# Attention and gated MLP on one core: a common PSUM pool, paced weight conversion, and unsplit float32 probabilities for the first 256 queries of each head in the first batch

## The chip, the cores and the metric

One core of a Trainium2 chip runs the whole program. The metric is device time in microseconds of one execution; lower is better. Engines are called PE (TensorE), DVE (VectorE), ACT (ScalarE), POOL (GpSimd) and SP (SyncE, which issues the DMAs); each works through its own list of instructions in order.

## What is computed

All inputs are float32 (the weights come as 64-bit numbers and are made float32 on the chip). Queries are averaged in pairs, so a head has 576 queries against 1152 keys of 64 elements.

```python
batch, n_heads, seq, head_dim = (4, 8, 1152, 64)
n_tokens, d_model, d_ff = (2304, 512, 1536)
q_pool = q.reshape(B, H, S // factor, factor, D).mean(axis=3)      # factor = 2
scores = scale * np.matmul(q_pool, k.transpose(0, 1, 3, 2))
scores = scores - np.max(scores, axis=-1, keepdims=True)
attn = np.exp(scores)
attn = attn / (np.sum(attn, axis=-1, keepdims=True) + 1e-09)
...                                          # x = attn @ v, heads side by side
gate = 1.0 / (1.0 + np.exp(-(x @ w_gate)))
return (gate * (x @ w_val)) @ w_out
```

## The kernel before, in words

**Precision by splitting.** A value is split into a rounded part (float32r) and the rest, and a product is made of several float32r matmuls: two for scores, two for a product with the values (the stationary operand `vt` holds the values' high and low parts side by side in 128 columns), three for the gated MLP. Splitting costs an ACT (or POOL) copy for the high part and a DVE or POOL subtraction for the low one.

**Steps of the attention.** Two heads are a pair (`p`, 16 pairs in 4 batches) and make nine steps (`STEPS`, L157), each a tile of 128 queries: four of the first head, one with 64 queries of each, four of the second. `PB` = 36 steps are a batch. A step (`scores`, L303) is: three cuts of the scores on PE (L326), the row maximum on DVE (L333), the exponential on ACT (L338) into `P`; then nine PE transposes in three groups (L367), each copied as its high part by ACT (L382) and subtracted for its low part by DVE (L386) into `pt`. When a head's 256 or 320 queries are there, `values` (L395) multiplies: 18 matmuls (L408); the halves in 64 partitions each are added by an ACT copy (L419) into `t` and a DVE addition (L422) into `y`. After a pair, `normalise` (L432) multiplies `y` by the inverse sums (DVE L464) and splits it into `x` (ACT L472, POOL L476). `head_operands` (L233) loads and splits q, k and v.

**PSUM.** Eight banks of 512 columns. In the first batch scores alternate between `S0` (banks 0, 1 and a quarter of 2) and `S1` (the rest of 2, bank 3, half of 4); later only `S0` is used. Transposes have the two banks `T` (6, 7), results of products have `m` (3, 4, 5), of which two are taken away (`blocked`) until the last exponential of the first batch.

**The rest.** `convert` (L483) makes float32 parts of a weight piece: a load on SP, ACT L493, DVE L497, L498, L503, ACT L507, POOL L510, a store to DRAM; 36 pieces, from the first steps on. `gated` (L527) of batch b runs beside the attention of batch b+1: 864 matmuls a batch (L541), with weights loaded back (L555, L601). The gated product of the first batch can't begin before the first batch's last `x` is there, so PE has nothing but attention until then.

**What sets the order.** Every piece is recorded as an operation with an engine, an assumed duration, a priority (about its step) and the buffers that it takes (`SLOTS` gives their number). `Plan.run` (L63) plays them against each other by the assumed durations: an engine that is free takes the operation of lowest priority number that could start. The resulting list is then written out, engine by engine; the assumed durations decide the order and nothing else.

Of the kernel before, what the change touches and what calls it, by code (L numbers as in the profile page):

```python
# [37 lines left out]
class Plan:  # L38


    LAT = {"PE": 0.22, "ACT": 0.12, "DVE": 0.12, "POOL": 0.15, "SP": 0.0}
# [21 lines left out]
    def run(self):  # L63
# [32 lines left out]
        while done < len(self.ops):  # L96
            if not times:
                left = sorted((o.key[0], o.eng) for e in ready for _, o in ready[e])
                raise RuntimeError(f"planner stuck at {t}: {left[:10]} {nxt}")
            t = heapq.heappop(times)  # L100
            while times and times[0] <= t + 1e-9:
                heapq.heappop(times)
            again = True
            while again:
                again = False
                for e in self.LAT:
                    if busy[e] > t + 1e-9:
                        continue
                    put, pick = [], None
# [39 lines left out]
def attention_glu_kernel(ctx: ExitStack, tc: tile.TileContext, qT, kT, vt_in, v, wg, wv, wo, out):  # L149
# [15 lines left out]
    }  # L165
    pl = Plan(SLOTS, ("m",))
# [5 lines left out]
    def tiles(tag, shape, dt, pool=const):  # L172
# [12 lines left out]
        "m": [bank[:, 512 * i:512 * i + 512] for i in (3, 4, 5)],  # L185
        "T": [bank[:, 512 * i:512 * i + 512] for i in (6, 7)],
# [10 lines left out]
        "g": tiles("g", [128, 2, HALF], F32R),  # L197
        "opart": tiles("opart", [128, HALF], F32),
# [6 lines left out]
    }  # L205
    w_d = {
# [11 lines left out]
    def act(n, extra=0):  # L218
        return 0.17 + 0.815e-3 * n + 0.093 * extra

    def dve(n):
        return 0.14 + 1.06e-3 * n

    def pool(n, two=True):
        return 0.2 + (2.4e-3 if two else 1.3e-3) * n

    def dma(kb):
        return 0.1 + kb / 250

    T_PE = 0.12  # L230


    def head_operands(u, need):  # L233
# [67 lines left out]
        return dict(k=kh, q=qh, v=vh, got=got, vg=vg)  # L301

    def scores(p, j, hd, st):  # L303
# [15 lines left out]
        cuts = ((0, 384), (384, 896), (896, SK)) if early and s % 2 else ((0, 512), (512, 1024), (1024, SK))  # L319
        for n, (a, b) in enumerate(cuts):  # L320

            def mm(a=a, b=b):
                t = tl(sh)
                seq = [(q, kk[w][:, a:b]) for w, q in lhs for kk in (KA, KB)]
                for n, (q, k) in enumerate(seq):
                    nc.tensor.matmul(out=t[:, a:b], lhsT=q, rhs=k, start=(n == 0), stop=(n == len(seq) - 1))  # L326

            mms.append(pl.op("PE", 2 * len(lhs) * pe(b - a), mm, s - 0.5, after=got if n == 0 else mms[-1:],
                             uses=uses + ([sh] if n else []), take=[] if n else [sh]))
# [12 lines left out]
        a = pl.op("DVE", dve(SK), rmax, s - 0.5, after=mms[-1:], uses=[sh])  # L342
# [4 lines left out]
        ex_op = pl.op("ACT", act(SK, 2), ex, s - 0.5, after=[a], uses=block + [sh] + ([] if j == 0 else [st["den"]]), take=take)  # L347
        st.setdefault("ex", []).append(ex_op)

# [7 lines left out]
        for w, g, _, _ in dst:  # L357
            if (w, g) not in st:
                st[w, g] = dict(h=pl.hold("pt"), ops=[])
                new.append(st[w, g]["h"])  # L360
        for n in range(3):
            th = pl.hold("T")
# [6 lines left out]
            a = pl.op("PE", 3 * T_PE, tr, s + 1 + 0.1 * n, after=[ex_op], uses=[ph], take=[th])  # L369
            for w, g, so, do in dst:  # L370
# [4 lines left out]
                def views(n=n, th=th, so=so, do=do, h=h, width=width):  # L375
                    src = tl(th)[:, 0:384].rearrange("p (c q) -> p c q", q=128)[:, :, so:so + width]
                    d = tl(h)[:, :, 3 * n:3 * n + 3, do:do + width]
                    return src, d[:, 0], d[:, 1]
# [9 lines left out]
                tk = [h] if h in new else []  # L388
                if tk:
                    new.remove(h)  # L390
                b = pl.op("ACT", act(3 * width), hi, s + 1 + 0.1 * n, after=[a], uses=[th] + ([] if tk else [h]), take=tk)
                b = pl.op("DVE", dve(3 * width), lo, s + 1 + 0.1 * n, after=[b], uses=[th, h])
                st[w, g]["ops"].append(b)

    def values(p, j, w, g, hd, st):  # L395
# [5 lines left out]
        m = pl.hold("m")  # L401
        last = None
        for n, (c0, c1) in enumerate(((0, 3), (3, 5), (5, 7), (7, 9))):

            def mm(c0=c0, c1=c1):
                for c in range(c0, c1):
                    for k in range(2):
                        nc.tensor.matmul(out=tl(m)[:, 0:N], lhsT=tl(hd[w]["v"])[:, c], rhs=tl(h)[:, k, c, 0:N],  # L408
                                         start=(c == 0 and k == 0), stop=(c == NC - 1 and k == 1))

            last = pl.op("PE", 2 * (c1 - c0) * pe(N), mm, s, after=st[w, g]["ops"] + [hd[w]["vg"]] + in_turn if n == 0 else [last],
                         uses=[h, hd[w]["v"]] + ([m] if n else []), take=[] if n else [m])
            if n == 0:
                in_turn[:] = [last]
        th = pl.hold("t")
        mine, other = slice(64 * w, 64 * w + 64), slice(64 - 64 * w, 128 - 64 * w)

# [5 lines left out]

        last = pl.op("ACT", act(N), cp, s, after=[last], uses=[m], take=[th])
        tk = []
        if "y" not in st:
            st["y"] = pl.hold("y")
            tk = [st["y"]]
        st.setdefault("yo", []).append(
            pl.op("DVE", dve(N), add, s, after=[last], uses=[m, th] + ([] if tk else [st["y"]]), take=tk))  # L430

    def normalise(p, st):  # L432
# [16 lines left out]
        ms = [pl.hold("m"), pl.hold("m")]  # L449
# [33 lines left out]
    def convert(kind, m, s, due):  # L483
# [11 lines left out]
        def bits():  # L495
            low, high = tl(cr)[:, :, 0], tl(cr)[:, :, 1]
            nc.vector.tensor_scalar(out=low, in0=low, scalar1=29, scalar2=None, op0=ALU.logical_shift_right)  # L497
# [18 lines left out]
        a = pl.op("SP", dma(512), load, due - 4, take=[cr], late=3.0)  # L516
        a = pl.op("ACT", act(512), scale, due, after=[a], uses=[cr])
        a = pl.op("DVE", 2 * dve(512), bits, due, after=[a], uses=[cr])
        a = pl.op("DVE", dve(512), join, due, after=[a], uses=[cr])
# [7 lines left out]
    def gated(b, xs):  # L527
        base = PB * (b + 1) + 2.5
# [3 lines left out]
        def product(at, w, parts, N, uses, after):  # L532

            m = pl.hold("m")
# [13 lines left out]
        for th in range(3):  # L548
            gs = {}
            for m_ in range(4 * th, 4 * th + 4):  # L550
# [7 lines left out]
                lw = pl.op("SP", dma(1024), load, at - 4, after=stored["wg", m_], take=[wh], late=3.0)  # L558
                for n in range(2):
                    sg, gh = pl.hold("sg"), pl.hold("g")  # L560
                    qc = slice(n * HALF, (n + 1) * HALF)
                    for s in range(2):
# [15 lines left out]
                        else:  # L578
# [13 lines left out]
                            a = pl.op("ACT", act(HALF), hi, at - 1, after=[a], uses=[sg], take=[gh])  # L592
                            a = pl.op("POOL", pool(HALF), lo, at - 1, after=[a], uses=[sg, gh])
                            gs[m_ % 4, n] = (gh, a)
            for dm in range(4):
# [8 lines left out]
                lw = pl.op("SP", dma(512), load, at - 4, after=stored["wo", m_], take=[wh], late=3.0)  # L604
                for n in range(2):
# [21 lines left out]
                    if th == 0:  # L627
                        a = pl.op("ACT", act(HALF), post, at - 1, after=[last], uses=[ms], take=[oh])
# [11 lines left out]
    in_turn = []  # L640
    acc = {}
    xs = {}
    blocked = [pl.hold("m"), pl.hold("m")]
    pl.op("SP", 0.0, lambda: None, -100, take=blocked)
    for b in range(B):
# [60 lines left out]
```

## Time and profile before

| | |
|---|---|
| runs before | 1060.4 us median of 3 (1058.04 to 1060.67) |
| profiled execution | 1058.06 us, of which the span of its instructions is 1056.2 us |
| PE busy | 981.1 us (93%), 6944 matmuls |
| DVE, ACT, POOL busy | 654.6 us (62%), 561.3 us (53%), 423.7 us (40%) |
| first row maximum, 36th row maximum, first gated matmul start at | 14.31 us, 198.46 us, 226.57 us |
| bytes moved by DMA | 166.33 MB, 157 GB/s in the mean |

Read it by stages: the shares over the span mix a stage in which PE waits with one in which it does not. A matmul's duration in the profile holds its way through the array, and matmuls overlap; what one costs in a run of them is the distance from one to the next, which the chain of waits shows as a piece's length over its count.

### The profile page before, as it was taken

The page shows a single profiled execution, that of the slowest core. Times are in us where ns is not written, and L with a number is a line of the kernel's source. Part 1 is how long each engine was busy: PE and PEld are TensorE (multiplying, and loading weights), DVE is VectorE, ACT ScalarE, POOL GpSimd, SP SyncE. Part 2 cuts the span into 40 slices and gives each one's busy share as a digit, 9 for nine tenths or more (in the row PEclk, how much of TensorE's full clock was granted, in tenths as well). Part 3 has the DMA queues.
Part 4 walks back from the last instruction along what each step waited for, and adds up shares of the span by engine and source line. Part 5 has one row for each costly group of instructions (what it writes and reads, how often), then busy time and mean ns, then how long its engine had stood idle before and what let it go on. Part 6 is the DMA issues. An engine that isn't in the chain of part 4 may idle for free.

```text
span 1056.2 us, 18322 instructions
## 1 busy us (share of the span) xinstructions
PE 981.1 (93%) x6944; PEld 931.3 (88%) x6944; DVE 654.6 (62%) x1086; ACT 561.3 (53%) x1179; POOL 423.7 (40%) x408
## 2 busy tenths in 40 slices
PE   4886777679999999999999999999999999999998
PEld 3675666569999999999999999999999999999998
DVE  4778887777778887865656665665656665530121
ACT  4657665566666656655555545545555545522211
POOL 6445544435646455624524434414524422111211
PEclk9889988999999999999999999999999999999999
DMA  6645555636777585874444352554444332255443
GB/s 164 188 145 168 146 165 149 162 129 198 224 240 229 164 238 173 266 239 136 137 125 136 116 157 103 153 154 136 137 125 137 121 108 80 87 159 168 170 175 92
DMA packets 53463, 166.33 MB, mean 157 GB/s; under 512 B 10368, under 2 KB 14464, under 8 KB 47232
## 3 DMA queue, kind: packets, MB, share of 16 engines
q1 hardware_dynamic: 53376, 165.18, 51.1%
q8 instruction: 54, 0.88, 0.4%
q14 instruction: 33, 0.27, 0.1%
HBM read 141.56 MB, written 23.59 MB: 156 GB/s over the span
## 4 chain that ended last, share of the span: by engine, by line
PE 76%; DVE 3%; ACT 1%; issue 1%; DMA 0%; ACTq 0%; DVEq 0%
PE bank L541 43%; PE bank L326 12%; PE bank L408 11%; PE bank L367 10%; PE bank L455 1%; DVE cr L503 1%; DVE cr L498 1%; DVE pt L386 1%; DVE nm L333 1%; ACT P L338 0%; ACT pt L382 0%; DVE cr L497 0%; DMA wo<-wo_d 0%; ACT cr L493 0%; DVE sg L581 0%
## 5 line engine op out<-in xcount | busy, mean ns | idle before, releaser
L541 PE MATMUL bank<-x,wg 128*128 128x288 f32 x2304 | 369.4, 303 | 0.0
L541 PEld LDWEIGHTS bank<-x,wg 128*128 128x128 f32 x2304 | 316.2, 188 | 0.1
L386 DVE TENSOR_TENSOR pt<-bank,pt 128x384 fp32r<-128x384 f32 (+1 forms) x480 | 233.1, 510 | 122.6 <-ACT pt L382 120.7
L382 ACT ACTIVATE pt<-bank 128x384 fp32r<-128x384 f32 (+1 forms) x480 | 206.9, 460 | 121.3 <-PE bank L367 115.1
L367 PE MATMUL bank<-ident,P 128*128 128x128 f32 x1296 | 214.1, 280 | 34.4 <-DVE pt L386 31.4
L333 DVE TENSOR_REDUCE nm<-bank 128x1 f32<-128x1152 f32 x144 | 195.1, 1355 | 63.4 <-PE bank L326 60.4
L367 PEld LDWEIGHTS bank<-ident,P 128*128 128x128 f32 x1296 | 161.0, 143 | 50.4 <-DVE pt L386 40.4
L326 PE MATMUL bank<-KA,Q 128*128 128x512 f32 (+3 forms) x480 | 177.5, 371 | 27.9 <-ACT P L338 12.5
L338 ACT ACTIVATE P<-bank,nm 128x1152 f32<-128x1152 f32 x144 | 175.8, 1221 | 50.5 <-DVE nm L333 43.0
L541 PE MATMUL bank<-g,wo 128*128 128x288 f32 x1152 | 183.8, 303 | 1.3 <-DMA wo<-wo_d 1.3
L588 POOL TENSOR_TENSOR g<-sg,g 128x288 fp32r<-128x288 f32 x96 | 77.5, 807 | 264.9 <-ACT g L585 259.3
L408 PE MATMUL bank<-pt,vt 128*128 128x256 f32 (+1 forms) x1152 | 168.8, 301 | 0.0
L326 PE MATMUL bank<-KB,Q 128*128 128x512 f32 (+3 forms) x480 | 165.9, 365 | 1.0 <-POOL KB L286 1.0
L541 PEld LDWEIGHTS bank<-g,wo 128*128 128x128 f32 x1152 | 158.6, 189 | 2.1 <-DVE opart L625 1.5
L408 PEld LDWEIGHTS bank<-pt,vt 128*128 128x128 f32 x1152 | 160.2, 193 | 0.1
L326 PEld LDWEIGHTS bank<-KA,Q 128*128 128x128 f32 x480 | 94.3, 196 | 47.0 <-ACT P L338 17.7
L326 PEld LDWEIGHTS bank<-KB,Q 128*128 128x128 f32 x480 | 94.8, 197 | 13.1 <-POOL KB L286 2.2
L581 DVE SCALAR_TENSOR_TENSOR sg<-sg,bank 128x288 f32<-128x288 f32 x96 | 43.3, 451 | 94.6 <-PE bank L541 93.2
L286 POOL TENSOR_TENSOR KB<-kr,KA 128x576 fp32r<-128x576 f32 x64 | 96.9, 1515 | 5.9 <-ACT KA L281 1.9
L575 ACT ACTIVATE sg<-bank 128x288 f32<-128x288 f32 x96 | 39.6, 412 | 106.8 <-PE bank L541 102.9
L510 POOL TENSOR_TENSOR cs<-cr,cs 128x512 fp32r<-128x512 f32 x36 | 50.9, 1415 | 92.3 <-ACT cs L507 88.5
L293 POOL CAST vt<-vr 128x576 fp32r<-128x576 f32 x32 | 23.1, 721 | 138.2 <-PE bank L408 138.2
(35 smaller groups left out, 613.0 us busy)
## 6 DMA issues: line engine op xcount, KB each, us to landing
wg<-wg_d SPq DMA_DIRECT2D x48, 1024.0 KB, 4.9
wo<-wo_d SPq DMA_DIRECT2D x48, 512.0 KB, 3.6
kr<-in_kT_dram SPq DMA_DIRECT2D x64, 288.0 KB, 5.1
wg_d<-cs SPq DMA_DIRECT2D x24, 512.0 KB, 6.0
qr<-in_qT_dram SPq DMA_DIRECT2D x32, 288.0 KB, 3.9
vr<-in_v_dram SPq DMA_DIRECT2D x32, 288.0 KB, 3.4
qr<-in_qT_dram SPq DMA_DIRECT2D x32, 256.0 KB, 3.6
cr<-in_wg_dram SPq DMA_DIRECT2D x12, 512.0 KB, 5.2
```

The lines of the kernel that those rows point to most:

```text
L286: nc.gpsimd.tensor_tensor(out=kb[:, s], in0=tl(kr)[:, s], in1=ka[:, s].bitcast(F32), op=ALU.subtract)
L326: nc.tensor.matmul(out=t[:, a:b], lhsT=q, rhs=k, start=(n == 0), stop=(n == len(seq) - 1))
L333: nc.vector.tensor_reduce(out=c, in_=tl(sh)[:, 0:SK], axis=AXX, op=ALU.max, negate=True)
L338: nc.scalar.activation(out=tl(ph), in_=tl(sh)[:, 0:SK], func=ACTF.Exp, bias=c, accum_out=tl(st["den"])[:, col:col + 1])
L367: nc.tensor.transpose(out=tl(th)[:, c * 128:(c + 1) * 128], in_=tl(ph)[:, k:k + 128], identity=ident)
L382: nc.scalar.activation(out=dh, in_=src, func=ACTF.Copy)
L386: nc.vector.tensor_tensor(out=dl, in0=src, in1=dh.bitcast(F32), op=ALU.subtract)
L408: nc.tensor.matmul(out=tl(m)[:, 0:N], lhsT=tl(hd[w]["v"])[:, c], rhs=tl(h)[:, k, c, 0:N], start=(c == 0 and k == 0), stop=(c == NC - 1 and ...
L510: nc.gpsimd.tensor_tensor(out=tl(cs)[:, 1], in0=tl(cr)[:, :, 0].bitcast(F32), in1=tl(cs)[:, 0].bitcast(F32), op=ALU.subtract)
L541: nc.tensor.matmul(out=ps[:, 0:N], lhsT=l, rhs=r, start=(n == 0 and j == 0), stop=(n == 3 and j == 2))
L581: nc.vector.scalar_tensor_tensor(out=tl(sg), in0=tl(sg), scalar=1.0, in1=tl(ms)[:, 0:HALF], op0=ALU.add, op1=ALU.mult)
L588: nc.gpsimd.tensor_tensor(out=tl(gh)[:, 1], in0=tl(sg), in1=tl(gh)[:, 0].bitcast(F32), op=ALU.subtract)
```

## The change

The planner's table of assumed durations is set anew, and a free engine other than PE now leaves an operation for a more urgent one that will be ready within 0.4 us (`WAIT`). PSUM: `T` and `m` become one pool `b` of banks 3 to 7 (two of them blocked in the first batch as before, so three are in use there); bank 2, which `S0` and `S1` share, is a buffer `b2` of its own, and a step on `S1` now makes its cut in bank 2 last. In the first batch the first 256 queries of each head (`g == 0`) keep their transposed probabilities unsplit in `pe` (float32): no low part is made, and the product is nine float32 matmuls with the raw values `vr` as the stationary operand (64 columns), whose result ACT copies straight into `y`. The other 320 queries, and all later batches, stay split. Weight pieces get later due steps in the first batch, and a load waits for the exponential eight steps ahead of its due step. `kr` and `vr` have two buffers; `x`, `g`, `sg` and `t` have one fewer, and `g` and `opart` take the place of `pe` after the first batch.

```diff
 class Plan:
+    WAIT = 0.4
...
+                        if t < o.at <= t + self.WAIT and can(o, o.at):
+                            soon.append(o)
                         put.append(it)
+                    if pick and e != "PE" and any(
+                        t + pick.dur > u.at + self.WAIT and u.prio < pick.prio - 0.3 for u in soon
+                    ):
+                        heapq.heappush(ready[e], it)
+                        pick = None
...
-        "S0": 1, "S1": 1, "T": 2, "m": 3, ... "P": 2, "pt": 2,
-        "vr": 1, "vt": 2, "y": 2, "t": 2, "rb": 1, "x": 7, "g": 9, ...
-        "cr": 2, "kr": 1, "cs": 1, "sg": 3, "den": 2,
+        "S0": 1, "S1": 1, "b2": 1, "b": 5, ... "P": 2, "pt": 2, "pe": 2,
+        "vr": 2, "vt": 2, "y": 2, "t": 1, "rb": 1, "x": 6, "g": 8, ...
+        "cr": 2, "kr": 2, "cs": 1, "sg": 2, "den": 2,
...
-        cuts = ((0, 384), (384, 896), (896, SK)) if early and s % 2 else ((0, 512), (512, 1024), (1024, SK))
+        cuts = ((384, 896), (896, SK), (0, 384)) if early and s % 2 else ((0, 512), (512, 1024), (1024, SK))
+        shared = [pl.hold("b2")] if early else []
...
-                st[w, g] = dict(h=pl.hold("pt"), ops=[])
+                st[w, g] = dict(h=pl.hold("pe" if s < PB and g == 0 else "pt"), ops=[])
...
+                b = pl.op("ACT", act(3 * width), hi, s + 1 + 0.1 * n, after=[a], uses=[th, h])
+                if h.tag == "pt":
+                    b = pl.op("DVE", dve(3 * width), lo, s + 1 + 0.1 * n, after=[b], uses=[th, h])
...
+        whole = h.tag == "pe"
+        vh = hd[w]["vr" if whole else "v"]
+        for n in range(NC):
+            def mm(c=n):
+                if whole:
+                    nc.tensor.matmul(out=tl(m)[0:D, 0:N], lhsT=tl(vh)[:, c], rhs=tl(h)[:, c, 0:N],
+                                     start=(c == 0), stop=(c == NC - 1))
+                else:
+                    for k in range(2):
+                        nc.tensor.matmul(out=tl(m)[:, 0:N], lhsT=tl(vh)[:, c], rhs=tl(h)[:, k, c, 0:N], ...)
...
+        def cp_whole():
+            nc.scalar.activation(out=tl(st["y"])[mine, a:b], in_=tl(m)[0:D, 0:N], func=ACTF.Copy)
...
         a = pl.op("SP", dma(512), load, due - 4, take=[cr], late=3.0)
+        gate.append((a, max(0, int(due) - AHEAD)))
...
-                    due = max(due, 6 + 2.5 * (k + 8 * th))
+                    due = max(due, 16 + 2.5 * (k + 8 * th))
...
+    for o, k in gate:
+        o.after.append(exs[k])
```

The order that comes out differs on every engine; two places follow. Names are tile and buffer number; `bank` is all of PSUM.

On PE, the first head's product of its first 256 queries. Before (`pt`, `vt`), between the scores of two steps:

```order
L326 MATMUL bank<-KB_69,Q_71 128x128
L408 MATMUL bank<-pt_76,vt_79 128x256 x18
L367 MATMUL bank<-ident,P_74 128x128 x6
L326 MATMUL bank<-KA_67,Q_71 128x384
L326 MATMUL bank<-KB_69,Q_71 128x384
L326 MATMUL bank<-KA_67,Q_71 128x512
```

With the change (`pe`, `vr`):

```order
L346 MATMUL bank<-KB_68,Q_70 128x256
L437 MATMUL bank<-pe_107,vr_79 64x256 x3
L346 MATMUL bank<-KA_66,Q_70 128x384
L346 MATMUL bank<-KB_68,Q_70 128x384
L437 MATMUL bank<-pe_107,vr_79 64x256 x6
L388 MATMUL bank<-ident,P_75 128x128 x6
```

It is nine instructions in place of 18, comes a step sooner (in the fourth step, not after the fifth), and is parted by the step's cut in bank 2 (128x384), which on this odd step now comes last.

On DVE, from the first row maximum (`nm`) on. Before:

```order
L333 TENSOR_REDUCE nm<-bank 128x1 x2
L503 SCALAR_TENSOR_TENSOR cr_114<-cr_114 128x512
L497 TENSOR_SCALAR cr_115<-cr_115 128x512
L498 SCALAR_TENSOR_TENSOR cr_115<-cr_115 128x512
L386 TENSOR_TENSOR pt_76<-bank,pt_76 128x3x128
L333 TENSOR_REDUCE nm<-bank 128x1
L270 SCALAR_TENSOR_TENSOR Q_71<-qr_73,Q_71 64x576
L386 TENSOR_TENSOR pt_76<-bank,pt_76 128x3x128 x2
```

With the change:

```order
L353 TENSOR_REDUCE nm<-bank 128x1 x2
L288 SCALAR_TENSOR_TENSOR Q_71<-qr_74,Q_71 64x576
L353 TENSOR_REDUCE nm<-bank 128x1 x2
L411 TENSOR_TENSOR pt_77<-bank,pt_77 128x3x128 x3
L353 TENSOR_REDUCE nm<-bank 128x1
L411 TENSOR_TENSOR pt_77<-bank,pt_77 128x3x128 x2
```

The low parts of the first two steps are gone, and so is the conversion of weights (`cr`), whose first piece now stands after the eleventh row maximum.

## Rows read from the trace of the kernel before

**Rows 1.** The page's busy time of each engine, with its share of the span and its number of instructions.

```profile
PE 981.1 (93%) x6944; PEld 931.3 (88%) x6944; DVE 654.6 (62%) x1086; ACT 561.3 (53%) x1179; POOL 423.7 (40%) x408
```

**Rows 2.** Windows: each stretch (us), its length, busy time of the engines in it with their instructions, PE's granted clock as a share of 2.4 GHz, busy share of the DMA engines, GB/s. The borders are the start of the first row maximum, of the 36th, and of the first gated matmul, then 262, 464 and 935 us.

```profile
0.00:14.31 14.31, 3.92 (x9) 2.59 (x10) 3.29 (x5) 4.62 (x6) 6.93 (x11) 1.00 0.88 227
14.31:198.46 184.15, 136.54 (x773) 114.87 (x773) 145.54 (x223) 112.37 (x226) 91.55 (x79) 0.89 0.53 153
198.46:226.57 28.11, 20.11 (x131) 17.42 (x131) 21.67 (x36) 17.87 (x36) 13.69 (x14) 0.98 0.63 175
226.57:262.00 35.43, 32.50 (x237) 30.98 (x237) 26.92 (x39) 21.43 (x46) 16.10 (x15) 1.00 0.56 159
262.00:464.00 202.00, 200.20 (x1464) 192.91 (x1463) 159.96 (x260) 128.52 (x266) 106.15 (x97) 1.00 0.71 223
464.00:935.00 471.00, 471.00 (x3459) 456.13 (x3458) 278.02 (x484) 252.54 (x545) 168.47 (x170) 1.00 0.42 129
935.00:1056.20 121.20, 116.85 (x881) 116.41 (x879) 19.16 (x42) 23.99 (x57) 20.80 (x25) 1.00 0.45 153
```

**Rows 3.** The timeline (start in us, length in us, engine, line, instruction): the first and the 36th row maximum on DVE, the last `y` of the first batch, the first gated matmuls.

```profile
14.31 2.64 DVE L333 TENSOR_REDUCE nm<-bank 128x1 f32<-128x1152 f32 x2 [1.40 <-PE bank L326]
198.46 1.36 DVE L333 TENSOR_REDUCE nm<-bank 128x1 f32<-128x1152 f32 x1 [0.75 <-PE bank L326]
222.98 1.11 DVE L464 TENSOR_TENSOR y<-y,bank 128x256 f32<-128x256 f32 x4
226.57 1.66 PE L541 MATMUL bank<-x,wg 128*128 128x288 f32 x11
```

**Rows 4.** Waits from 14.31 to 198.46 us: who waited for whom, us in total, times, the longest.

```profile
ACT pt L382 <- PE bank L367: 39.1, 33, 3.2
PEld bank L367 <- DVE pt L386: 29.0, 33, 4.0
PE bank L367 <- DVE pt L386: 22.1, 18, 3.8
DVE nm L333 <- PE bank L326: 16.3, 15, 2.6
DVE pt L386 <- ACT pt L382: 14.0, 14, 1.4
PE bank L326 <- ACT P L338: 10.3, 12, 2.5
```

**Rows 5.** Instructions of DVE and ACT from 14.31 to 198.46 us by line and shape: busy us, mean ns of one, then the idle time before them and what ended it.

```profile
L333 DVE TENSOR_REDUCE nm<-bank 128x1 f32<-128x1152 f32 x35 | 47.3, 1353 | 18.6 <-PE bank L326 16.3 <-ACT P L338 2.2
L386 DVE TENSOR_TENSOR pt<-bank,pt 128x384 fp32r<-128x384 f32 x85 | 44.7, 549 | 11.0 <-ACT pt L382 10.3
L503 DVE SCALAR_TENSOR_TENSOR cr<-cr 128x512 uint32<-128x512 uint32 x14 | 13.5, 962 | 0.2
L498 DVE SCALAR_TENSOR_TENSOR cr<-cr 128x512 uint32<-128x512 uint32 x13 | 12.2, 941 | 1.1
L422 DVE TENSOR_TENSOR y<-bank,t 64x256 f32<-64x256 f32 x7 | 2.9, 418 | 0.9 <-ACT t L419 0.7
L422 DVE TENSOR_TENSOR y<-bank,t 64x320 f32<-64x320 f32 x6 | 2.9, 488 | 2.2 <-ACT t L419 2.2
L382 ACT ACTIVATE pt<-bank 128x384 fp32r<-128x384 f32 x85 | 40.0, 490 | 36.8 <-PE bank L367 36.4
L419 ACT ACTIVATE t<-bank 64x256 f32<-64x256 f32 x7 | 2.7, 380 | 3.5 <-PE bank L408 3.4
```

**Rows 6.** Pieces of the chain of waits, in order of time: start, length, what. A run of matmuls of one line is one piece: 18 of 320 columns twice, 12 of the gated product, 18 of 256 columns, three transposes.

```profile
198.43 3.31 PE bank L408 x18
...
208.95 2.65 PE bank L408 x18
...
231.17 1.59 PE bank L541 x12
232.75 2.17 PE bank L408 x18
...
248.42 0.33 PE bank L367 x3
```

**Rows 7.** The products with the values over the whole span: matmuls and their weight loads (count, busy us, mean ns of one, idle before).

```profile
L408 PE MATMUL bank<-pt,vt 128*128 128x256 f32 (+1 forms) x1152 | 168.8, 301 | 0.0
L408 PEld LDWEIGHTS bank<-pt,vt 128*128 128x128 f32 x1152 | 160.2, 193 | 0.1
```

**Rows 8.** The timeline around one odd step on `S1`: the exponential of the step before, the cut in bank 2 that waits for it, the last cut, the row maximum.

```profile
40.24 1.22 ACT L338 ACTIVATE P<-bank,nm 128x1152 f32<-128x1152 f32 x1 [0.69 <-DVE nm L333]
...
41.61 0.44 PE L326 MATMUL bank<-KA,Q 128*128 128x384 f32 x1 [0.39 <-ACT P L338]
41.89 0.34 PE L326 MATMUL bank<-KB,Q 128*128 128x384 f32 x1
...
42.65 0.31 PE L326 MATMUL bank<-KB,Q 128*128 128x256 f32 x1
...
43.09 1.35 DVE L333 TENSOR_REDUCE nm<-bank 128x1 f32<-128x1152 f32 x1
```

More of the change, by code (lines that the diff above doesn't have):

```diff
@@ L108, in run @@
                         continue
-                    put, pick = [], None
+                    put, pick, soon = [], None, []
                     while ready[e]:
@@ L184, in attention_glu_kernel @@
         "S1": [bank[:, SK:2 * SK]],
-        "m": [bank[:, 512 * i:512 * i + 512] for i in (3, 4, 5)],
-        "T": [bank[:, 512 * i:512 * i + 512] for i in (6, 7)],
+        "b": [bank[:, 512 * i:512 * i + 512] for i in (3, 4, 5, 6, 7)],
         "kr": tiles("kr", [128, SK], F32),
@@ L205, in attention_glu_kernel, with change_pools @@
     }
+    late = ctx.enter_context(ExitStack())
+    early = ctx.enter_context(ExitStack())
+    TL["pe"] = tiles("pe", [128, NC, 256], F32, early.enter_context(tc.tile_pool(name="pe", bufs=1)))
+    def change_pools():
+        early.close()
+        pool = late.enter_context(tc.tile_pool(name="late", bufs=1))
+        TL["g"] = tiles("g", [128, 2, HALF], F32R, pool)
+        TL["opart"] = tiles("opart", [128, HALF], F32, pool)
     w_d = {
@@ L341, in scores @@
         block = [] if not early else [blocked[0], blocked[1]]
-        a = pl.op("DVE", dve(SK), rmax, s - 0.5, after=mms[-1:], uses=[sh])
+        a = pl.op("DVE", dve(SK), rmax, s - 0.5, after=mms[-1:], uses=[sh] + shared)
         take = [ph]
@@ L346, in scores @@
             take.append(st["den"])
-        ex_op = pl.op("ACT", act(SK, 2), ex, s - 0.5, after=[a], uses=block + [sh] + ([] if j == 0 else [st["den"]]), take=take)
+        ex_op = pl.op("ACT", act(SK, 3.3), ex, s - 0.5, after=[a], uses=block + shared + [sh] + ([] if j == 0 else [st["den"]]), take=take)
         st.setdefault("ex", []).append(ex_op)
+        exs.append(ex_op)
         dst = []
@@ L367, in tr @@
                     nc.tensor.transpose(out=tl(th)[:, c * 128:(c + 1) * 128], in_=tl(ph)[:, k:k + 128], identity=ident)
-            a = pl.op("PE", 3 * T_PE, tr, s + 1 + 0.1 * n, after=[ex_op], uses=[ph], take=[th])
+            old = [st[w, g]["h"] for w, g, _, _ in dst if st[w, g]["h"] not in new]
+            a = pl.op("PE", 3 * T_PE, tr, s + 1 + 0.1 * n, after=[ex_op], uses=[ph] + old, take=[th] + new)
+            new = []
             for w, g, so, do in dst:
@@ L400, in values @@
         h = st[w, g]["h"]
-        m = pl.hold("m")
+        m = pl.hold("b")
         last = None
-        for n, (c0, c1) in enumerate(((0, 3), (3, 5), (5, 7), (7, 9))):
-            def mm(c0=c0, c1=c1):
-                for c in range(c0, c1):
+        tk = []
+        if "y" not in st:
+            st["y"] = pl.hold("y")
+            tk = [st["y"]]
+        whole = h.tag == "pe"
[6 more added lines that the diff above has]
+                else:
                     for k in range(2):
-                        nc.tensor.matmul(out=tl(m)[:, 0:N], lhsT=tl(hd[w]["v"])[:, c], rhs=tl(h)[:, k, c, 0:N],
+                        nc.tensor.matmul(out=tl(m)[:, 0:N], lhsT=tl(vh)[:, c], rhs=tl(h)[:, k, c, 0:N],
                                          start=(c == 0 and k == 0), stop=(c == NC - 1 and k == 1))
-            last = pl.op("PE", 2 * (c1 - c0) * pe(N), mm, s, after=st[w, g]["ops"] + [hd[w]["vg"]] + in_turn if n == 0 else [last],
-                         uses=[h, hd[w]["v"]] + ([m] if n else []), take=[] if n else [m])
+            last = pl.op("PE", N / 600 + 0.08 if whole else 2 * pe(N), mm, s, after=st[w, g]["ops"] + [hd[w]["vg"]] + in_turn if n == 0 else [last],
+                         uses=[h, vh] + ([m] if n else []), take=[] if n else [m] + tk)
             if n == 0:
                 in_turn[:] = [last]
-        th = pl.hold("t")
+        th = None if whole else pl.hold("t")
         mine, other = slice(64 * w, 64 * w + 64), slice(64 - 64 * w, 128 - 64 * w)
+        if whole:
+            last_whole[:] = [last]
         def cp():
@@ L422, in add @@
             nc.vector.tensor_tensor(out=tl(st["y"])[mine, a:b], in0=tl(m)[mine, 0:N], in1=tl(th)[mine, 0:N], op=ALU.add)
+        def cp_whole():
+            nc.scalar.activation(out=tl(st["y"])[mine, a:b], in_=tl(m)[0:D, 0:N], func=ACTF.Copy)
+        if whole:
+            st.setdefault("yo", []).append(
+                pl.op("ACT", act(N), cp_whole, s, after=[last], uses=[m] + [st["y"]]))
+            return
         last = pl.op("ACT", act(N), cp, s, after=[last], uses=[m], take=[th])
[L425 to L428, printed above, removed]
         st.setdefault("yo", []).append(
-            pl.op("DVE", dve(N), add, s, after=[last], uses=[m, th] + ([] if tk else [st["y"]]), take=tk))
+            pl.op("DVE", dve(N), add, s, after=[last], uses=[m, th] + [st["y"]]))
     def normalise(p, st):
@@ L527, in gated @@
     def gated(b, xs):
+        if not switch:
+            switch.append(pl.op("SP", 0.0, change_pools, PB + 1, after=last_whole))
         base = PB * (b + 1) + 2.5
@@ L532, in product @@
         def product(at, w, parts, N, uses, after):
-            m = pl.hold("m")
+            m = pl.hold("b")
             last = None
@@ L556, in load @@
                                       in_=w_d["wg"][m_].rearrange("p h s f -> p h (s f)"))
-                lw = pl.op("SP", dma(1024), load, at - 4, after=stored["wg", m_], take=[wh], late=3.0)
+                lw = pl.op("SP", dma(1024), load, at - 4, after=stored["wg", m_], take=[wh], late=1.5)
                 for n in range(2):
@@ L591, in gated @@
                             a = pl.op("DVE", dve(HALF), post, at - 1, after=[last, tanh], uses=[ms, sg])
-                            a = pl.op("ACT", act(HALF), hi, at - 1, after=[a], uses=[sg], take=[gh])
+                            a = pl.op("ACT", act(HALF), hi, at - 1, after=[a] + switch, uses=[sg], take=[gh])
                             a = pl.op("POOL", pool(HALF), lo, at - 1, after=[a], uses=[sg, gh])
@@ L602, in load @@
                                       in_=w_d["wo"][m_].rearrange("p h s f -> p h (s f)"))
-                lw = pl.op("SP", dma(512), load, at - 4, after=stored["wo", m_], take=[wh], late=3.0)
+                lw = pl.op("SP", dma(512), load, at - 4, after=stored["wo", m_], take=[wh], late=1.5)
                 for n in range(2):
@@ L627, in gated @@
                     if th == 0:
-                        a = pl.op("ACT", act(HALF), post, at - 1, after=[last], uses=[ms], take=[oh])
+                        a = pl.op("ACT", act(HALF), post, at - 1, after=[last] + switch, uses=[ms], take=[oh])
                     else:
```

43 lines of the change are left out of this document (21 added, 22 removed), and 4 rows, old and new, of the table SLOTS.

## The prediction

> **What bounds the kernel now.** I read the busy shares first, then windows by stage, then the waits of the first stage. The shares say that PE is busy 93% of the span [rows 1], which hides two different kernels. From 262 us to 935 us PE is busy 671.2 of 673 us: there the time is PE's work, and nothing but PE's work can change it. Ahead of the first gated matmul at 226.57 us [rows 3] PE is busy 3.92 + 136.54 + 20.11 = 160.6 us [rows 2], and even that counts matmuls at their full length. So PE is idle for 66 us, and since all that follows is PE-bound, **the end moves by as much as the first gated matmul moves** (its distance to the end is the same PE work, as far as the later batches are unchanged).
>
> What sets the 226.57 us? From the first to the 36th row maximum there are 35 steps in 184.15 us, 5.26 us a step. DVE is busy 145.54 us of them (79%), PE 136.54 (74%), ACT 112.37 (61%), POOL 91.55 (50%) [rows 2]. No engine is full; it is a ring of waits in which DVE carries most: transposes wait for the low parts to free a bank (29.0 us at the weight loads), ACT waits for transposes (39.1), DVE for scores (16.3) and for ACT's copies (14.0) [rows 4]. The reader is to see that shortening DVE's part helps twice: DVE has less to do, and the bank of a transpose comes free after ACT's copy alone.
>
> **The change, part by part.**
>
> *Low parts gone.* Eight heads lose six subtractions of 384 columns each; by the order, 37 of the 48 stand ahead of the 36th row maximum (85 before, 48 now), the rest after it. 37 x 0.549 = 20.3 us. The addition into `y` goes too: seven of 0.418 us, 2.9 us [rows 5]. ACT keeps its copies: the copy of the product goes into `y` instead of `t`, one for one (0.380 us), and the copy of the probabilities stays (0.490 us): nothing.
>
> *Paced weights.* Before the 36th row maximum DVE issues two of L503 and one of L498 fewer: 2 x 0.962 + 0.941 = 2.9 us [rows 5]; one more addition of 320 columns gives 0.5 back. The pieces are not fewer, they come later. By the order all 36 stand ahead of the 73rd row maximum, as before, and at the 49th as many are done (21), so I see no new lateness and cost this at nothing; what covers it is a lead of about a dozen pieces at the first gated matmul. On SP a load now waits for an exponential, and the loads of q, k and v are queued behind it; `kr` and `vr` with two buffers cover that.
>
> DVE in the 35 steps: 145.5 - 20.3 - 2.9 - 2.9 + 0.5 = 119.9 us, 3.43 us a step.
>
> *The unsplit product.* Out go 144 matmuls of 256 columns at 2.17 / 18 = 0.121 us [rows 6], 17.4 us in all. In come 72 of float32, of which no row shows one. From below: three transposes, which also read unsplit float32, take 0.33 us, 0.11 us for 128 columns; 256 columns would be 0.22 us. From above: a weight load and a matmul one after the other, 0.193 + 0.301 = 0.49 us [rows 7]. I take 0.49: the transpose only moves data and already goes at half the rate of a float32r matmul, while a product must also do the four partial products that the split spreads over 128 stationary columns and two matmuls. So PE gets 72 x 0.49 - 17.4 = +17.9 us in the first batch (between -1.6 and +17.9), or 4.4 us in place of 2.2 for a product. (The Trainium skill, FP8 and Floating Point Precision, section TensorE Precision Notes, says that true FP32 takes four passes through the array; that speaks against this change, and by it one matmul would be an estimated 4 x 0.121 = 0.48 us and the sum +17.3 us. No run so far shows it.) PE's idle 66 us hide this, but not fully: a product of 4.4 us stands in order before a step's scores or transposes.
>
> *The cut in bank 2 last.* On the odd step of [rows 8] the exponential ends at 41.46 us, all three cuts follow, and the row maximum starts at 43.09, 1.63 us later. With two cuts done ahead only the 384 columns remain, whose second matmul starts at 41.89; a maximum follows the start of the last matmul by 43.09 - 42.65 = 0.44 us, so it would start at 42.33, 0.87 us after the exponential. That is some 0.7 us for each of 18 odd steps, at most 13 us, taken out of the 16.3 us in which DVE waits for scores.
>
> *Common banks.* Three banks are in use in the first batch as before, now for anything. A gain without a number; zero in the sum.
>
> *Later batches.* One buffer fewer of `x`, `g`, `sg`, `t`. From 262 us on PE idles 1.8 us until 464 and not at all until 935 [rows 2]; the order of gated products against scores is the same there within a row. Zero; if that cover went, each us of PE idle would be one at the end.
>
> *The sum.* 35 steps: DVE's busy time 119.9 us plus its idle time. That was 184.15 - 145.54 = 38.6 us; I take off 8 of the 13 us of the bank-2 cut and put on 14 of the 16 us that the 63 unsplit matmuls ahead of the 36th maximum add to PE (63 x (0.49 - 2 x 0.121) = 15.7): 44.6 us. Together 164.5 us, 19.7 less, 4.7 us a step. From the 36th row maximum to the first gated matmul there were 28.11 us with DVE busy 21.67; 12 low parts (6.6 us) go and the last product, which is on the path, is 2.2 us longer: 23.7 us, 4.4 less. The sum is 24.1 us. The profiled execution took 1058.06 us (span 1056.2), so 1034 us; the median of the runs shown is 1060.4, 2.3 above, which is a spread I cannot place, so 1034 stands.
>
> **The rivals.**
>
> *A, the ring opens.* DVE and ACT keep PE fed, and the pace falls to where DVE is at its old 79%: 119.9 / 0.79 = 152 us, with the tail in proportion (22), or below. 14.3 + 152 + 22 = 188 us, 38 us gained, 1020; the floor is PE's own busy time, 160.6 + 17.9 = 178.5, which is 1000 once its clock is whole. For it: the clock was 0.89 over the 184.15 us, 0.11 / 0.5 x 184 = 40 us at 1.2 instead of 2.4 GHz, and the same 18 matmuls took 3.31 us at 198.43 and 2.65 us at 208.95 [rows 2, 6]. A PE with fewer holes might keep 2.4 GHz. (The Trainium skill, TensorE: Matmul & The Clock Gate, Part 1, has it that half rate is the default and activity releases it; the trace agrees as far as the half-rate stretches all lie in the stage with idle PE.) Against: three engines near the same load always wait for each other.
>
> *B, PE becomes the bound (slower).* If one unsplit matmul costs more than I allow, PE's list fills the first stage. PE would need 160.6 - 17.4 + 72 p us, with about 10 us before it starts; that reaches 226.6 at p = (226.6 - 10 - 143.2) / 72 = 1.02 us. At p = 1.2 us the first gated matmul comes 13 us later: 1071. Four partial products at the half clock (4 x 2 x 0.121 = 0.97) come close to that. Against: PE would have to be busy all the time at the low clock.
>
> *C, the loop alone decides.* Row maximum, exponential, cut in bank 2, row maximum: if waits and not DVE's load make the 5.26 us, the freed DVE time turns idle and the end stays at 1058. For: 1.35 + 1.22 + 0.9 + signals is 3.6 us and each engine's other work delays each link. Against: the waits for low parts are the largest ones of PE.
>
> **How the numbers follow.** My forecast of 1034 stands for its own range of 1020 to 1048: 0.56. A, 1000 to 1020: 0.22. B, above 1061: 0.12. C, within a few us of 1058: 0.10. About 0.3% (3.2 us) is what a measurement here can tell from no change. The range that leaves out the lower end of A and most of B is 1008 to 1058. Faster by over 0.3% are the forecast, A and a part of C's spread: 0.80; within: 0.07; slower: 0.13.
>
> **What would show it.** Right: first gated matmul near 202 us; the 36th row maximum near 179; about 4.7 us a step; DVE busy near 120 us in those steps; unsplit matmuls 0.4 to 0.5 us apart; PE full from about 225 us on; the distance from the first gated matmul to the end as before, 829.6 us within 3. Wrong: unsplit matmuls at 1 us or more, transposes queued behind them; a first gated matmul near 226 with DVE idle; or PE waiting for `wg`, `wo` or `x` after it, which would say that the smaller buffers or the later weights took the gain back.

## The result and the profile after

The change makes the kernel **faster**: 1033.23 us median (1030.99 to 1035.71) against 1060.42, ratio 0.9749, 95% interval 0.9723 to 0.9775. The profiled execution took 1035.71 us, its span 1033.1.

Windows of the kernel after, with the same borders as [rows 2] (first row maximum, 36th, first gated matmul, then three of the later stage); columns as there:

```profile
0.00:13.39 13.39, 3.16 (x7) 1.84 (x8) 0.94 (x3) 3.22 (x4) 5.99 (x11) 1.00 0.87 202
13.39:181.62 168.23, 141.85 (x811) 111.64 (x811) 128.36 (x178) 117.06 (x234) 91.40 (x80) 0.98 0.60 172
181.62:202.01 20.39, 17.21 (x93) 13.51 (x92) 18.06 (x24) 12.28 (x25) 12.75 (x12) 0.83 0.65 193
202.01:237.00 34.99, 34.51 (x249) 32.86 (x247) 28.03 (x45) 23.73 (x53) 16.10 (x16) 1.00 0.64 193
237.00:436.00 199.00, 195.28 (x1429) 188.69 (x1428) 163.41 (x252) 126.95 (x262) 107.94 (x97) 1.00 0.75 232
436.00:912.00 476.00, 475.03 (x3494) 461.29 (x3493) 285.54 (x491) 254.20 (x548) 169.94 (x172) 1.00 0.40 125
912.00:1033.10 121.10, 116.06 (x874) 115.39 (x872) 18.81 (x42) 23.89 (x56) 19.92 (x25) 1.00 0.44 151
```

The 35 steps take 168.23 us, 4.81 each (5.26 before); the first gated matmul starts 24.6 us sooner (226.57 before); from it to the end there are 831.1 us (829.6 before). All of the gain lies ahead of the first gated matmul. The two rows that answer to [rows 3], from the timeline:

```profile
181.62 1.35 DVE L353 TENSOR_REDUCE nm<-bank 128x1 f32<-128x1152 f32 x1
202.01 1.82 PE L586 MATMUL bank<-x,wg 128*128 128x288 f32 x12
```

Waits between the first and the 36th row maximum, as [rows 4]:

```profile
ACT P L358 <- DVE nm L353: 24.7, 22, 4.9
DVE nm L353 <- PE bank L346: 21.6, 14, 4.4
PEld bank L346 <- ACT P L358: 20.5, 22, 2.2
PEld bank L388 <- DVE pt L411: 9.9, 11, 2.8
PE bank L388 <- DVE pt L411: 7.0, 8, 2.3
ACT pt L407 <- PE bank L388: 6.8, 11, 1.1
```

Transposes wait for DVE a third as long as before (29.0 and 22.1 us [rows 4]). What waits now is one ring: exponential for row maximum, row maximum for scores, scores for exponential. How a step looks in the timeline, here row maxima and exponentials of the seventh to ninth step:

```profile
39.37 1.35 DVE L353 TENSOR_REDUCE nm<-bank 128x1 f32<-128x1152 f32 x1
40.81 1.22 ACT L358 ACTIVATE P<-bank,nm 128x1152 f32<-128x1152 f32 x1 [1.75 <-DVE nm L353]
44.07 1.35 DVE L353 TENSOR_REDUCE nm<-bank 128x1 f32<-128x1152 f32 x1
45.72 1.22 ACT L358 ACTIVATE P<-bank,nm 128x1152 f32<-128x1152 f32 x1
47.63 1.36 DVE L353 TENSOR_REDUCE nm<-bank 128x1 f32<-128x1152 f32 x1 [0.82 <-PE bank L346]
```

Each exponential follows its own maximum, and the next maximum comes after it. In the kernel before, the same seventh step:

```profile
38.80 1.35 DVE L333 TENSOR_REDUCE nm<-bank 128x1 f32<-128x1152 f32 x1
44.54 1.22 ACT L338 ACTIVATE P<-bank,nm 128x1152 f32<-128x1152 f32 x1 [0.35 <-DVE nm L333]
```

Its exponential comes 5.74 us after its maximum starts; the eighth step's maximum, at 43.09 [rows 8], runs ahead of it and ends at 44.44, and the exponential starts 0.1 us after that. So it is in 17 of the first 35 steps of the kernel before: the exponential starts less than 0.1 us after the end of the next step's maximum, in the mean 3.3 us after its own. These are the 17 times in this row of the waits from 14.31 to 198.46 us, which [rows 4] leaves out:

```profile
ACT P L338 <- DVE nm L333: 12.8, 17, 4.2
```

The two neighbours have bank 2 and the tile `nm` in common; for which of them the exponential waits, the trace does not say. With the change no exponential waits for the next step's maximum. Over the 36 steps of the first batch, the mean from the start of a maximum to the end of its exponential is 6.34 us before and 2.70 after.

The unsplit products, all instructions of their line (durations in ns: shortest, median, longest):

```profile
L437 PE MATMUL bank<-pe,vr x144: 379/379/689, 23.5 to 198.1; 128*64 128x256 f32 x144
```

72 matmuls make 144 records, whose starts are mostly 0.216 us apart: 0.43 us a matmul, and nine in a row are one piece of the chain. The last nine of the batch are the second piece below:

```profile
65.91 4.03 PE bank L437 x18
192.71 5.74 PE bank L437 x18
```

The granted clock rose in the steps (0.98, before 0.89) and fell ahead of the first gated matmul (0.83, before 0.98). PE stood idle for 3.2 us before 190.32 us, the clock from 190 to 195 us was 0.50, that is 1.2 GHz, and the last nine matmuls began there. The higher clock of the steps is not needed for their length: one version below (split and apart) takes the same time for them at 0.93.

### The profile page after: what moved, and what is told of

It reads as the page before. It is cut to its first block, busy times and chain, and to the rows that moved or that the text cites. A ratio compares the mean times of both kernels' runs of the same rounds, so it can differ in the third digit from the quotient of the medians.

```text
span 1033.1 us, 18159 instructions
## 1 busy us (share of the span) xinstructions
PE 983.1 (95%) x6944; PEld 925.2 (90%) x6944; DVE 643.1 (62%) x1030; ACT 561.3 (54%) x1179; POOL 424.0 (41%) x408
## 4 chain that ended last, share of the span: by engine, by line
PE 80%; DVE 7%; DMA 3%; ACT 2%; issue 2%; POOL 1%; SPq 0%; DVEq 0%; ACTq 0%; POOLq 0%
PE bank L586 42%; PE bank L346 14%; PE bank L441 12%; PE bank L388 10%; DVE nm L353 2%; PE bank L437 2%; ACT P L358 1%; DVE pt L411 1%; DMA wo<-wo_d 1%; DVE cr L539 1%; PE bank L493 1%; DVE cr L544 1%; DMA cr<-in_wg_dram 1%; DVE cr L535 1%; DMA wg_d<-cs 1%
## 5 line engine op out<-in xcount | busy, mean ns | idle before, releaser
L586 PE MATMUL bank<-x,wg 128*128 128x288 f32 x2304 | 379.0, 304 | 0.3 <-DVE y L457 0.3
L411 DVE TENSOR_TENSOR pt<-bank,pt 128x384 fp32r<-128x384 f32 (+1 forms) x432 | 203.1, 506 | 42.4 <-ACT pt L407 41.0
L388 PE MATMUL bank<-ident,P 128*128 128x128 f32 x1296 | 207.1, 275 | 9.2 <-DVE pt L411 7.0
L407 ACT ACTIVATE pt<-bank 128x384 fp32r<-128x384 f32 (+1 forms) x432 | 182.3, 456 | 57.8 <-PE bank L388 53.6
L346 PE MATMUL bank<-KA,Q 128*128 128x512 f32 (+3 forms) x480 | 171.3, 359 | 27.1 <-ACT P L358 17.6
L586 PE MATMUL bank<-g,wo 128*128 128x288 f32 x1152 | 186.9, 303 | 5.8 <-DVE pt L411 3.0
L346 PE MATMUL bank<-KB,Q 128*128 128x512 f32 (+3 forms) x480 | 159.1, 358 | 0.8 <-POOL KB L304 0.7
L441 PE MATMUL bank<-pt,vt 128*128 128x320 f32 (+1 forms) x1008 | 147.9, 300 | 3.5 <-DVE pt L411 3.5
L441 PEld LDWEIGHTS bank<-pt,vt 128*128 128x128 f32 x1008 | 140.5, 191 | 4.7 <-ACT pt L407 4.4
L301 POOL CAST KA<-kr 128x576 fp32r<-128x576 f32 x62 | 48.5, 783 | 65.5 <-PE bank L346 65.5
```

Of the source, the lines that this page charges most:

```text
L301: nc.gpsimd.tensor_copy(ka[:, s], tl(kr)[:, s])
L388: nc.tensor.transpose(out=tl(th)[:, c * 128:(c + 1) * 128], in_=tl(ph)[:, k:k + 128], identity=ident)
L407: nc.scalar.activation(out=dh, in_=src, func=ACTF.Copy)
L411: nc.vector.tensor_tensor(out=dl, in0=src, in1=dh.bitcast(F32), op=ALU.subtract)
L441: nc.tensor.matmul(out=tl(m)[:, 0:N], lhsT=tl(vh)[:, c], rhs=tl(h)[:, k, c, 0:N], start=(c == 0 and k == 0), stop=(c == NC - 1 and k == 1))
L586: nc.tensor.matmul(out=ps[:, 0:N], lhsT=l, rhs=r, start=(n == 0 and j == 0), stop=(n == 3 and j == 2))
```

## The experiments

Theory 1 was the prediction's: the low parts on DVE set the pace. Times and ratios are medians of all executions, ratios to the kernel before in the same session; the columns from "us a step" on are of the one profiled execution. "In steps" is from the first to the 36th row maximum.

| kernel | us | ratio [95%] | us a step | first gated | from there to the end | DVE, PE busy in steps | maximum to end of exponential |
|---|---|---|---|---|---|---|---|
| before | 1060.4 | 1 | 5.26 | 226.6 | 829.6 | 145.5, 136.5 | 6.34 |
| the change | 1033.2 | 0.9749 [0.9723, 0.9775] | 4.81 | 202.0 | 831.1 | 128.4, 141.8 | 2.70 |
| split again | 1036.6 | 0.9801 [0.9771, 0.9832] | 4.75 | 202.7 | 830.1 | 143.9, 132.4 | 2.76 |
| unsplit alone | 1052.7 | 0.9938 [0.9914, 0.9962] | 5.11 | 215.8 | 836.2 | 118.5, 151.8 | 4.95 |
| bank 2 first | 1043.2 | 0.9840 [0.9804, 0.9875] | 4.93 | 206.8 | 835.1 | 129.0, 141.9 | 2.69 |
| weights early | 1038.4 | 0.9806 [0.9786, 0.9827] | 5.02 | 204.9 | 831.3 | 137.8, 146.2 | 2.73 |
| old durations | 1033.6 | 0.9769 [0.9750, 0.9789] | 4.60 | 195.4 | 836.5 | 123.4, 137.1 | 2.70 |
| product twice | 1060.7 | 1.0021 [1.0005, 1.0038] | 5.55 | 230.8 | 832.3 | 129.3, 170.7 | 2.71 |
| ballast, PSUM | 1039.7 | 0.9807 [0.9775, 0.9839] | 4.92 | 201.6 | 836.7 | 145.7, 143.4 | 2.72 |
| ballast, SBUF | 1045.1 | 0.9872 [0.9840, 0.9904] | 5.05 | 210.0 | 836.8 | 153.8, 143.3 | 2.70 |
| banks apart | 1031.8 | 0.9749 [0.9719, 0.9779] | 4.87 | 202.2 | 827.0 | 126.9, 144.2 | 2.74 |
| no bank-2 buffer | 1043.3 | 0.9846 [0.9831, 0.9861] | 5.09 | 207.9 | 834.1 | 123.9, 148.8 | 4.16 |
| common banks alone | 1047.3 | 0.9877 [0.9858, 0.9897] | 4.89 | 204.7 | 841.9 | 140.1, 136.0 | 4.10 |
| split and apart | 1033.3 | 0.9753 [0.9721, 0.9785] | 4.81 | 200.1 | 833.7 | 143.9, 134.2 | 2.75 |

**Split again.**

```diff
-                st[w, g] = dict(h=pl.hold("pe" if s < PB and g == 0 else "pt"), ops=[])
+                st[w, g] = dict(h=pl.hold("pt"), ops=[])
```

> The changed kernel with the probabilities of all queries split again in the first batch (pools, bank-2 cut, pacing and planner stay). Theory 1 (DVE's low parts set the first batch's pace): DVE gets 37 x 0.55 + 2.9 = 23 us back in the 35 steps, PE sheds 72 x 0.43 - 17.4 = 13.6 us; first gated matmul 12 to 22 us later than 202 us, about 219, and 1050 us in all. Theory 2 (pools, cut and planner made the gain, the product paid for itself at best): within 5 us of 1033.

Theory 1 fails: DVE has its 15.5 us back and the steps are no longer. At most a few us at the end are the unsplit product's. The run takes two things back at once, since PE also sheds 9.4 us in the steps; what DVE's part alone costs, the ballast below shows.

**Unsplit alone**, the same product put into the kernel before (`vr` 2, `x` 6).

> The kernel before with the unsplit product of the first 256 queries alone (old pools, cuts, planner and weights; vr has two buffers and x six, g and opart take the place of pe). Theory 1: most of the gain is here, first gated matmul 12 to 22 us earlier than 226.6 us, 1038 to 1048 us. Theory 2: 1055 to 1062 us, since PE's longer product stands in the way of the next step's scores under the old order.

7 us: between both. DVE's busy time in the steps fell by 27 us and PE's rose by 15; the first gated matmul comes 10.7 us sooner, just under Theory 1's 12, and 6.5 us are lost behind it.

**Bank 2 first.**

```diff
-        cuts = ((384, 896), (896, SK), (0, 384)) if early and s % 2 else ...
+        cuts = ((0, 384), (384, 896), (896, SK)) if early and s % 2 else ...
...
```

The buffer `b2` is then taken with that first cut.

> The changed kernel with the cut in bank 2 first again on odd steps. Theory 1: 8 of 13 us come back, since other waits cover the rest: 1041 us, even and odd steps differ in the distance from exponential to row maximum by 0.7 us. Theory 3 (the ring of row maximum, exponential and cut alone sets the pace): the full 18 x 0.76 = 13 us or more, 1047 us. If the cut's place is hidden anyway: 1033 us.

10 us, 5 of them ahead of the first gated matmul; odd steps take 2.59 us from the end of an exponential to the next maximum instead of 2.06, even ones 1.85 instead of 2.15.

**Weights early.**

```diff
-                    due = max(due, 16 + 2.5 * (k + 8 * th))
+                    due = max(due, 6 + 2.5 * (k + 8 * th))
...
-    for o, k in gate:
-        o.after.append(exs[k])
```

> The changed kernel with the old due steps of the weight pieces and without the wait for an exponential. Theory 1: 2 or 3 pieces more ahead of the 36th row maximum are 2.6 us of DVE each, of which about half shows: 1033 to 1038 us. If pacing matters by more than its DVE time (collisions early in the ring, the head of the first heads' loads): 1045 us or more.

5 us, the upper end; the first gated matmul comes 2.9 us later.

**Old durations**: `dve`, `pool`, `dma`, `T_PE`, the exponential's price and `late` as before, no look-ahead.

> The changed kernel with the planner's old durations and without the look-ahead. Theory 1: the lists change little where it matters, 1033 to 1040 us. Theory 2 (the planner made the gain): 1050 us or more.

The planner's prices are not the gain: the first gated matmul comes even 6.6 us sooner, and 5.4 us are lost behind it.

**Product twice.**

```diff
+                    for k in range(2):
                         nc.tensor.matmul(out=tl(m)[0:D, 0:N], lhsT=tl(vh)[:, c], rhs=tl(h)[:, c, 0:N],
-                                     start=(c == 0), stop=(c == NC - 1))
+                                     start=(c == 0 and k == 0), stop=(c == NC - 1 and k == 1))
```

> The changed kernel with every unsplit matmul issued twice (its result is then twice as large), the order unchanged: the price of one goes from 0.43 to 0.86 us, 31 us more of PE in the first batch. Theory 1: PE has 26 us without work in the 35 steps, so PE becomes the bound and about two thirds of it show: first gated matmul 15 to 25 us later, 1048 to 1058 us. If PE's part is hidden: under 1040 us. If every us of the product is on the path: 1064 us.

28.8 of 31 us at the first gated matmul, nearly all. PE's window in the 35 steps:

```profile
13.30:207.70 194.40, 170.79 (x938) 129.66 (x938) 129.40 (x178) 117.24 (x234) 92.05 (x80) 0.97 0.51 148
```

PE is busy 88% there and adds what it is given; the gain is gone at 0.86 us a matmul. Rival B's mechanism is real, and nearer than its 1.02 us.

**Ballast on DVE**, from PSUM and from SBUF.

```diff
+                if h.tag == "pe":
+                    def ballast(views=views, h=h, n=n, do=do):
+                        src, dh, _ = views()
+                        nc.vector.tensor_tensor(out=TL["bal"]..., in0=src, in1=dh, op=ALU.subtract)
+                    pl.op("DVE", dve(3 * width), ballast, s + 1 + 0.1 * n, after=[b], uses=[th, h])
```

> The changed kernel with the 48 subtractions of low parts back on DVE, reading the transpose's bank as before, their result not used; the product stays unsplit. DVE has 26 us more and the bank of a transpose waits for DVE again. Theory 1: 15 to 25 us, 1048 to 1058 us. Theory 3 (the ring alone): under 1040 us.

> The same 48 subtractions on DVE, but reading SBUF, so that the bank comes free after ACT's copy. If DVE's load is what counts: as the run that reads the bank, within 4 us. If the bank that is held until DVE has passed is what counts: near 1036 us while the other is at 1048 or more.

From PSUM: 26.6 us more of DVE, 17.3 of them net in the steps, which get 4.0 us longer; the stretch from the 36th maximum on is shorter (16.0 us at a clock of 1.00, against 20.4 at 0.83), so the first gated matmul is where it was (201.6), and the 6 us are lost behind it. From SBUF, 25.4 us more of DVE make the steps 8.4 us longer. So a quarter to a third of DVE's time shows in the steps: it is not free, but it does not set the pace as Theory 1 has it. The pair tells nothing about the bank, since the second one's instructions became longer; both, shortest, median and longest in ns:

```profile
L420 DVE TENSOR_TENSOR bal<-bank,pe x48: 544/558/559, 20.2 to 194.9; 128x384 fp32r<-128x384 f32 x48
```

```profile
L420 DVE TENSOR_TENSOR bal<-pe x48: 498/559/1624, 20.8 to 203.9; 128x384 fp32r<-128x384 f32 x48
```

**Banks apart** (`T` 2 and `m` 3 in place of `b` 5, the rest of the change stays), **no bank-2 buffer** (`shared = []`), and **common banks alone** (`b` 5 in the kernel before).

> The changed kernel with transposes in their own two banks and products and inverse sums in the other three (one usable in the first batch) as before; all else of the change stays. Since undoing the unsplit product cost only 3 us, Theory 2 has it that the pools made the gain. Theory 2a (the common banks: a transpose finds one of three, so the exponential no longer waits for the P buffer): 1048 to 1056 us and the time from the start of a row maximum to the end of its exponential, 6.3 us before and 2.7 us after, back above 4.5 us. Theory 2b (the buffer for bank 2 brings the list of ACT into another order, whatever the banks): within 5 us of 1033, and 2.7 us as it was.

> The changed kernel without the buffer for bank 2: the last cut of a step need not wait for the exponential of the step before, only for that of two steps before. Theory 2a: 2.1 us from the end of an exponential to the next row maximum is now the largest part of a step's 4.8 us; without the wait it goes below zero and the pace falls to what DVE, ACT and PE take, 4.3 us, 1015 to 1025 us. Theory 2b: row maximum and exponential part again (above 4.5 us) as in the kernel before, and the time goes towards 1050 us.

> The kernel before with the one pool of five banks in place of two and three, and nothing else of the change. Theory 2a: 1040 to 1048 us, most of the 23 us that the change makes without its unsplit product. Theory 2b: 1055 to 1062 us, and row maximum to exponential stays near 6.3 us.

The common banks bring 22 us to the first gated matmul when alone, lose 12 behind it in the profiled execution (13 us in all by the medians), and are worth nothing inside the change. The buffer for bank 2 is worth 10 us. Taking it away does not take the waits away. Neighbouring steps then still wait for each other, in another order. Here are the sixth to the eighth step of its timeline with the cuts in bank 2, and a row of its waits:

```profile
39.91 1.36 DVE L353 TENSOR_REDUCE nm<-bank 128x1 f32<-128x1152 f32 x1 [1.16 <-ACT P L358]
41.30 1.22 ACT L358 ACTIVATE P<-bank,nm 128x1152 f32<-128x1152 f32 x1 [0.46 <-DVE nm L353]
42.67 0.33 PE L346 MATMUL bank<-KA,Q 128*128 128x128 f32 x1 [0.33 <-ACT P L358]
43.21 1.36 DVE L353 TENSOR_REDUCE nm<-bank 128x1 f32<-128x1152 f32 x1 [0.43 <-PE bank L346]
44.62 0.44 PE L346 MATMUL bank<-KA,Q 128*128 128x384 f32 x1 [0.76 <-DVE nm L353]
44.90 0.34 PE L346 MATMUL bank<-KB,Q 128*128 128x384 f32 x1
45.28 1.22 ACT L358 ACTIVATE P<-bank,nm 128x1152 f32<-128x1152 f32 x1 [1.56 <-PE bank L346]
```

```profile
ACT P L358 <- PE bank L346: 15.4, 12, 2.2
```

The seventh step's cut in bank 2 (42.67) still waits for the sixth step's exponential. The eighth step's (44.62) waits only for the seventh step's maximum and goes ahead of its exponential, which then waits for that cut (45.28). An exponential waits for PE's scores 12 times here, and never in the kernels that have the buffer. So neighbouring steps wait for each other on bank 2 with or without the buffer; the buffer tells the planner of it, and the planner then puts a step's exponential ahead of the next step's cut in bank 2. The hope of 1015 to 1025 us without the wait was wrong.

**Split and apart**: both edits at once.

> The changed kernel with both undone at once: probabilities split again in the first batch, and transposes in two banks apart from the rest. Undone alone, the one cost 3 us and the other nothing; done alone in the kernel before, they brought 7 and 13 us. Theory 4 (both relieve the same thing, a transpose that waits for a bank until DVE has passed, so either is enough): 1044 to 1054 us, with transposes waiting for DVE as long as before (over 25 us at the weight loads). Theory 5 (neither matters once bank 2 has its buffer and the weights are paced): within 5 us of 1036.

Theory 5. Its steps, and its waits in them:

```profile
13.30:181.60 168.30, 134.28 (x809) 115.32 (x810) 143.91 (x228) 117.01 (x234) 92.11 (x80) 0.93 0.60 175
```

```profile
PEld bank L389 <- DVE pt L412: 35.9, 31, 2.2
PE bank L389 <- DVE pt L412: 28.1, 24, 2.0
ACT pt L408 <- PE bank L389: 25.0, 32, 2.2
```

DVE is as busy as before (143.9 us), transposes wait for it longer than before (35.9 against 29.0 at the weight loads), and the 35 steps take 168.3 us, as with the whole change. The waits that I took for the cause cost nothing in a kernel that has the rest of the change. In the kernel before they may have cost something: there the unsplit product and the common banks, each alone, brought the first gated matmul 10.7 and 21.8 us sooner, and each also let fewer exponentials wait for the next step's maximum (7 and 2 of 35, from 17).

## Why the prediction came out right, and where it was wrong

The number held (1034 forecast, 1033.2 measured), and so did its first step: **the end moves with the first gated matmul** (202.0 us against "near 202"; 24.6 us gained against a sum of 24.1; 831.1 us from there to the end). That distance held for the whole change, but not in general: over the runs it is 827.0 to 841.9 us, and PE's idle time behind the first gated matmul goes from 9.1 us before and 10.2 after to 14.0 (ballast, PSUM) and 14.7 (common banks alone); why was not tested. That the sum came out so close is luck: the 35 steps gave 15.9 us instead of 19.7, the stretch after them 7.7 instead of 4.4, and the first maximum came 0.9 us sooner. (Of the low parts of 384 columns that stretch lost 10, not 12: 14 before, 4 after.) The pace (4.81 against 4.7) and the 36th row maximum (181.6 against 179) came near, but the reason for them did not hold.

- *"DVE carries most."* Wrong. The low parts' removal was the largest term of the sum (20.3 us of DVE), and undoing it costs 3.4 us by the medians, together with the common banks nothing; 17.3 us of DVE put back alone cost 4.0 us of the steps. I had read the longest waits of PE [rows 4] as the ones that decide.
- *The unsplit product.* 0.43 us, between the bounds 0.22 and 0.49 and near the end that I took; 13.6 us more of PE instead of 17.9. (The four passes of the Trainium skill's FP8 and Floating Point Precision, section TensorE Precision Notes, are near it: 0.43 us is 3.6 times the 0.121 us of a float32r matmul.)
- *The cut in bank 2.* Misread. In [rows 8] the exponential at 40.24 us is that of the sixth step, and the cut at 41.61 belongs to the eighth: it waits for the exponential of two steps before, which read the same `S1`, and not for that of the step before, as I had it. What the buffer took away lay elsewhere: exponentials that waited for the next step's maximum (17 of 35). The term (8 us) has the size of what was measured (10 us for the cut's place, 10 for the buffer) for another reason: with the buffer, exponentials follow their own maxima at once.
- *Paced weights.* 2.9 us of DVE forecast, none came: 37 instructions of the conversion took 34.6 us of DVE in the steps, and 40 took 34.1 before. Undoing the pacing costs 5 us all the same.
- *Common banks: zero.* As forecast inside the change; alone they are worth 13 us. The planner's durations, which the sum leaves out, are worth nothing inside it.
- *DVE's busy time.* 119.9 us forecast, 128.4 measured; the low parts fell as forecast (19.9 us), the conversions and the scaling of `Q` (10.7 us, before 8.0) took longer.

Of the rivals, C was right that DVE's load does not decide, and wrong that the change leaves the waits alone; and the waits of the kernel before were not only those of its ring. Of B, PE's work does lie in the ring, since what is added to it shows nearly in full. A's hope for the clock came true in part (0.98 in the steps), but the time did not fall to its 1020 us.

**Left open:** which parts make the 24.6 us together. What is shown is that the rest of the change makes them without the unsplit product and without the common banks. Removed one by one, the buffer for bank 2 (10 us) and the pacing (5 us) do not add up to 27 us; at the first gated matmul they are 5.8 and 2.9 us. No run puts the buffer, the cut's place or the pacing alone into the kernel before, and the second buffers of `kr` and `vr`, and the parts in other pairs, were not tried. That the parts stand in for each other because each keeps exponentials from waiting for the next step fits the counts above and the last column of the table, but is argued and not shown: the order of the lists was not varied apart from the buffers.

## What to carry to other kernels

A long wait is a cause only if taking it away moves the end: undo each part of a change alone, then the parts that could stand in for each other together. Look, too, at what an instruction starts right behind: here half of the exponentials started 0.1 us after the next step's maximum, a wait of 12.8 us that the longest rows hid. Where a planner with fixed lists sets the order, a buffer that tells it of a wait that is there anyway can be worth more than the arithmetic saved, since it changes what every engine does first. A right total proves no term of its sum.

## What the runs showed of the hardware

An unsplit float32 matmul (64 stationary, 256 moving columns) is two records 0.216 us apart, and 0.427 us where the granted clock was 0.50. A DVE subtraction of 384 columns took 0.544 to 0.559 us with one input in PSUM. With both in SBUF, the 24 during which POOL ran nothing took 0.544 to 0.560 us, and the 24 beside an instruction of POOL 0.498 to 1.624 us, 1.00 in the mean. The Trainium skill (SBUF — State Buffer, section Who interferes with whom) says that a DVE instruction with two SBUF inputs contends with a GpSimd instruction that reads SBUF; the two rows of the ballast agree.
